# Sparse attention and gated feed-forward: block sums of the values on TensorE in column groups, a reordered start, other slots, stores on another queue

## Chip, cores, metric

One core of a Trainium2 chip runs the whole program. The metric is the device time of a run in microseconds (us); less is better. A ratio is the mean time of one kernel's fast runs over that of the kernel before in the same rounds on the same chip, so it is not quite the ratio of the medians that are quoted beside it.

In the profiles PE stands for TensorE's matmuls, PEld for its weight loads, DVE for VectorE, ACT for ScalarE, POOL for GpSimd, SP for SyncE; SPq and ACTq are instructions that start a DMA. L347 is a line of the kernel, x13 a number of instructions, and [2.30 <-DVE vx L427] says that the engine stood idle for 2.30 us and what ended it. The granted clock is the share of full TensorE speed that the chip allowed. PSUM is the memory that matmuls write to. A column group is the set of 32 of its 128 partitions that a small matmul writes to.

## The reference, cut to what matters

```python
batch, n_heads, seq, head_dim = (4, 8, 768, 64)
block, window = (32, 16)
k_sum = k.reshape(B, H, nb, block, D).max(axis=3)
v_sum = v.reshape(B, H, nb, block, D).mean(axis=3)        # block means: 24 per head
# scores: 15 neighbours on each side, and 24 block keys; one softmax over both
v_all = np.concatenate([v, v_sum], axis=2)
x = softmax(scores) @ v_all                               # -> 3072 tokens x 512
gate = 1.0 / (1.0 + np.exp(-(x @ w_gate)))
out = (gate * (x @ w_val)) @ w_out                        # d_ff = 1536
```

## The kernel before

Four batches go through one pipeline. While TensorE runs the feed-forward of batch b (24 units of 8 matmuls, then 12 output units of 6), the attention of batch b + 1 is put between its units: a text such as `6 Z0` means "after unit 6, do step Z of head pair 0". Each engine has one list of instructions, in the order of the program, so an instruction that waits can hold back those behind it on its engine (in the prediction's lines one wait stops all matmuls for 4.94 us). The step letters that matter here: T transposes keys and queries, K takes the key maxima (and spreads the keys), Z/S scores, A values, H halo copies, B spreads the block sums, D transposes by DMA.

```python
def sums(self, p, fill=0):          # batch 0: block sums on TensorE, all in column group 96:128
    vsp = self.vsp = ps([128, 512], FP32, "vsp")
    self.warm(vsp[:, 256:384], fill)            # fillers
    for t in range(NQ + 1):
        u = 2 * NQ * p + t
        nc.tensor.matmul(out=vsp[96:128, 0:128]..., lhsT=zband[0:64, 30 - 2 * t:62 - 2 * t],
                         rhs=self.vx[0:64, u:u + NQ + 1:NQ, 0:64], start=(t == 0), stop=(t == NQ))

def L(self, g, h=None, queue=None):  # batches 1 to 3: load the same values again, in fp32
    st = self.vm[g] = big()[0:4 * NS]
    (queue or nc.sync).dma_start(out=st, in_=v[self.b, 4 * g:4 * g + 4].rearrange(...))

def G(self, g, h):                   # ... reduce them on VectorE, put the result back by a small DMA
    nc.vector.tensor_reduce(out=self.mb[:, 32 * h:32 * h + 32], in_=self.vm[g]..., axis=AX.X, op=ALU.add)
    if h == 1:
        nc.sync.dma_start(out=self.heads(4 * g, 4 * g + 4, 0, 1, self.vx[96:120, ...]), in_=self.mb)

def m1(self, f, hf, c0=0, c1=NP):    # one feed-forward unit
    ...                              # 4 matmuls into gp, 4 into vp; four PSUM tiles: two units
    nc.scalar.activation(out=gate, in_=gp, func=ACT.Tanh, scale=0.5)
    nc.vector.scalar_tensor_tensor(out=self.hT[hf][:, f, :], in0=gate, scalar=1.0, in1=vp, ...)
...
NEXT = """
    3 T0   4 T1   5 Z0   6 T2   7 Z1   8 T3   9 G0a   10 Z2 G0b   11 G1a   12 Z3 G1b   13 H0 H1
    15 B0   16 B1   18 A0 A1   19 A2 A3 X0   20 X1   21 X2   22 X3"""
LATER = """
    0 G0a   1 G0b   2 K0   3 G1a   4 K1   5 G1b   6 Z0   8 K2 H0   10 Z1 H1   12 K3 B0   14 Z2 B1
    18 Z3   24 A0 A1   25 Y0   26 Y1   27 A2 A3   28 Y2   29 Y3"""
```

The start (batch 0 before its first complete feed-forward units) stands in an order of its own, with filler matmuls on a constant tile wherever TensorE would wait.

The softmax here doesn't subtract the row's maximum and nothing guards it: scores larger than these inputs give would overflow.

## Time and profile before

Median 261.63 us of three runs (259.44 to 261.75). The profiled span is 257.4 us. To compare kernels I cut the span at marks that can be read in the TensorE timeline: the end of the second complete feed-forward unit, and the first feed-forward matmul of the second half of batch 0 (45.32), of batch 1 (91.13), of batch 2 (151.66) and of batch 3 (206.60).

| stage, kernel before | us |
|---|---|
| start, to the end of two units | 26.21 |
| rest of batch 0's first half | 19.11 |
| batch 0, second half and output | 45.81 |
| batch 1 | 60.53 |
| batch 2 | 54.94 |
| batch 3 and end | 50.76 |

Batch 3 has no attention beside it: 46.9 us are matmuls without a wait, 3.9 us the last copy and store. Batches 1 and 2 carry some 3.6 us more matmuls, and no such end. The lines that carry the rest are in the prediction. The start, where fillers (L340) stand between the value steps (start, length, line, shapes):

```profile
15.21 0.90 PE L347 MATMUL vsp<-vx,zband 64*32 64x128 bf16 x13
16.04 0.38 PE L392 MATMUL av<-vs,P 24*64 24x64 bf16 x12
16.35 0.38 PE L377 MATMUL av<-vx,P 120*64 120x65 bf16 x12
16.66 0.62 PE L340 MATMUL last<-blank 128*128 128x128 bf16 x8
```

The fillers do nothing for the result. They take the place of idle time, and the granted clock is 1.00 through the start from its first record, at 3.94 us (before that 36 fillers come about 100 ns apart, later ones 57).

### The profile page before, as it was taken

The numbers are of one execution on the slowest core, as the hardware profiler recorded it, in microseconds if no ns is written. First come the engines' busy times: TensorE is split into PE (matmuls) and PEld (weight loads), VectorE is DVE, ScalarE is ACT, GpSimd is POOL, SyncE is SP. The second block draws the span as 40 slices with busy tenths as digits, with TensorE's granted clock in tenths as the row PEclk, the third lists the DMA queues.
The fourth block names the chain that finished last, engine by engine and source line by source line (L and its number), as shares of the span: only waits on it lengthen the run. The fifth ranks groups of instructions, "written<-read, shape, count | busy, mean of one in ns | idle before, by whom it ended". The sixth has DMA issues, their size and how long they took to land.

```text
span 257.4 us, 5546 instructions
## 1 busy us (share of the span) xinstructions
PE 239.9 (93%) x2290; PEld 137.8 (54%) x2290; DVE 149.8 (58%) x281; ACT 110.1 (43%) x193; POOL 65.4 (25%) x83
## 2 busy tenths in 40 slices
PE   8999999999996983998999999799999999999994
PEld 7687555566533541555555455455554456655441
DVE  7734857378997407999854219999654024444000
ACT  6833696488610450354541133455512233333111
POOL 8966434133899350262000000000000000000000
PEclk9999999999997997799999999999999999999999
DMA  7999999999999997999994963220006410000132
GB/s 186 147 158 196 203 204 222 221 167 126 125 125 160 166 228 169 161 177 162 133 87 80 173 173 105 35 63 3 1 3 175 122 72 0 3 0 0 43 122 82
DMA packets 87409, 30.74 MB, mean 119 GB/s; under 512 B 74520, under 2 KB 83736, under 8 KB 86808
## 3 DMA queue, kind: packets, MB, share of 16 engines
q0 software_dynamic: 62848, 15.37, 85.0%
q1 hardware_dynamic: 24536, 15.02, 27.5%
q8 instruction: 18, 0.29, 0.5%
q14 instruction: 7, 0.06, 0.1%
HBM read 33.08 MB, written 6.29 MB: 153 GB/s over the span
## 4 chain that ended last, share of the span: by engine, by line
PE 65%; DVE 14%; DMA 9%; issue 5%; ACT 4%; POOL 1%; SPq 1%; DVEq 0%; ACTq 0%; POOLq 0%
PE gp L498 18%; PE m L515 18%; PE vp L498 18%; DVE mb L417 4%; DMA vm<-in_v_dram 4%; DVE hT L506 3%; DVE P L327 2%; DMA k<-in_k_dram 2%; DMA vx<-mb 2%; ACT P L326 2%; PE av L444 2%; PE sc L320 2%; PE tp L205 2%; PE vsp L347 1%; PE last L340 1%
## 5 line engine op out<-in xcount | busy, mean ns | idle before, releaser
L506 DVE SCALAR_TENSOR_TENSOR hT<-gate,vp 128x384 bf16<-128x384 f32 x96 | 51.7, 549 | 59.1 <-PE vp L498 54.1
L498 PE MATMUL vp<-xT,wv 128*128 128x384 bf16 x384 | 80.1, 331 | 4.9 <-DVE hT L506 4.9
L498 PE MATMUL gp<-xT,wg 128*128 128x384 bf16 x384 | 80.3, 330 | 3.7 <-DVE hT L506 3.4
L505 ACT ACTIVATE gate<-gp 128x384 f32<-128x384 f32 x96 | 47.2, 493 | 64.2 <-PE gp L498 36.6
L515 PE MATMUL m<-wo,hT 128*128 128x512 bf16 x288 | 65.6, 384 | 0.0
L498 PEld LDWEIGHTS <-wv 128*128 128x128 bf16 x384 | 38.0, 99 | 30.9 <-issue 7.0
L498 PEld LDWEIGHTS <-wg 128*128 128x128 bf16 x384 | 36.0, 98 | 30.2 <-issue 8.4
L515 PEld LDWEIGHTS <-hT 128*128 128x128 bf16 x288 | 27.8, 99 | 32.1 <-issue 1.1
L520 ACT ACTIVATE ot<-m 128x512 f32<-128x512 f32 x24 | 14.3, 597 | 54.4 <-PE m L515 54.4
L417 DVE TENSOR_REDUCE mb<-vm 96x32 bf16<-96x1024 f32 x12 | 22.7, 1888 | 5.2 <-DMA vm<-in_v_dram 5.2
L326 ACT ACTIVATE P<-sc 128x768 bf16<-128x768 f32 x28 | 21.4, 812 | 6.1 <-PE sc L320 6.1
L161 POOL DMA_DIRECT2D vx<-in_v_dram x18 | 18.3, 1033 | 7.4 <-DMA nat<-in_q_dram 3.1
L155 POOL DMA_DIRECT2D nat<-in_q_dram x16 | 13.7, 857 | 21.6 <-DMA nat<-in_q_dram 12.7
L252 DVE TENSOR_REDUCE kTx<-kTn 128x24 bf16<-128x768 bf16 x16 | 15.1, 944 | 3.6 <-ACT kTn L210 3.6
L327 DVE TENSOR_TENSOR P<-P,mask 128x768 bf16<-128x768 bf16 x28 | 14.7, 550 | 3.3 <-ACT P L326 2.8
L155 POOL DMA_DIRECT2D nat<-in_k_dram x16 | 13.6, 853 | 9.9 <-DVE hT L506 3.7
L453 DVE TENSOR_TENSOR xs<-av,rec 128x768 bf16<-128x768 f32 (+1 forms) x16 | 13.7, 857 | 0.5
L444 PE MATMUL av<-vx,P 120*64 120x65 bf16 x336 | 8.2, 203 | 3.7 <-DVE vx L427 2.3
L444 PEld LDWEIGHTS <-P 120*64 120x64 bf16 x336 | 6.8, 117 | 7.7 <-issue 5.1
L474 ACT COPY xT<-br 128x384 bf16<-128x384 bf16 (+1 forms) x12 | 6.8, 587 | 9.5 <-PE br L471 9.5
L367 DVE COPY vx<-vx 32x792 bf16<-32x792 bf16 (+1 forms) x14 | 9.8, 705 | 0.3
L340 PEld LDWEIGHTS <-blank 128*128 128x128 bf16 x110 | 7.8, 111 | 2.4 <-DVE blank L567 1.1
(78 smaller groups left out, 140.2 us busy)
## 6 DMA issues: line engine op xcount, KB each, us to landing
out_dram<-ot SPq DMA_DIRECT2D x24, 256.0 KB, 2.1
vm<-in_v_dram SPq DMA_DIRECT2D x4, 768.0 KB
vx<-in_v_dram POOLq DMA_DIRECT2D x14, 192.0 KB, 14.7
wo<-in_moe_w_out_dram POOLq DMA_DIRECT2D x3, 512.0 KB, 21.0
vm<-in_v_dram POOLq DMA_DIRECT2D x2, 768.0 KB, 20.0
nat<-in_k_dram POOLq DMA_DIRECT2D x16, 96.0 KB, 10.8
nat<-in_q_dram POOLq DMA_DIRECT2D x16, 96.0 KB, 11.3
nat<-in_q_dram POOLq DMA_DIRECT2D x3, 384.0 KB, 14.0
```

What stands on the lines that cost most here:

```text
L155: nc.gpsimd.dma_start(out=nat[:, h // 2, :, 64 * (h % 2):64 * (h % 2) + 64], in_=tap[b, h].rearrange("(c p) d -> p c d", p=128))
L161: nc.gpsimd.dma_start(out=vx_t[b % 2][r0:r1, u0:u1, 0:64], in_=rows_of(v[b, 0, 0:1], (QT * u0 - 16 + r0) * D, [[D, r1 - r0], [QT * D, u1 - ...
L252: nc.vector.tensor_reduce(out=self.kTx[p][:, t, W:KX], in_=self.kTn[p][:, 16:16 + S].rearrange("p (n w) -> p n w", w=32), axis=AX.X, op=AL ...
L326: nc.scalar.activation(out=Ph, in_=sc[:, :, 0:6 * QT], func=ACT.Exp, scale=SCALE)
L327: nc.vector.tensor_tensor(out=Ph, in0=Ph, in1=mask[:, None, 6 * hf:6 * hf + 6, :].rearrange("p i t w -> p i (t w)") .to_broadcast([128, 2, ...
L417: nc.vector.tensor_reduce(out=self.mb[:, 32 * h:32 * h + 32], in_=self.vm[g].rearrange("p (w d) -> p d w", w=32)[:, 32 * h:32 * h + 32], a ...
L444: nc.tensor.matmul(out=av[r:r + 64, t // 6, (t % 6) // 2, i, 0:65], lhsT=P[0:KX, i, t, :], rhs=vx[0:KX, NQ * (2 * p + i) + t, 0:65], start ...
L498: nc.tensor.matmul(out=o, lhsT=wb[:, c, 128 * f:128 * (f + 1)], rhs=self.xT[:, c, HALF * hf:HALF * (hf + 1)], start=(c == 0), stop=(c == N ...
L505: nc.scalar.activation(out=gate, in_=gp, func=ACT.Tanh, scale=0.5)
L506: nc.vector.scalar_tensor_tensor(out=self.hT[hf][:, f, :], in0=gate, scalar=1.0, in1=vp, op0=ALU.add, op1=ALU.mult)
L515: nc.tensor.matmul(out=self.m3, lhsT=self.hT[hf][:, f, 128 * tt:128 * (tt + 1)], rhs=wo_bf[:, f], start=(f == 0), stop=(f == NF - 1))
L520: nc.scalar.mul(out=ot, in_=self.m3, mul=0.5)
```

## The change

The intent: no second, fp32 load of the values and no reduction on VectorE; all block sums as small matmuls in several column groups of TensorE at once; the value work of the first half batch between later scores in place of fillers; stores issued by ScalarE, so that SyncE's queue holds only transposes; the last tile in two halves. The diff, cut to its core (declarations and the order of some loads left out):

```diff
-        def L(self, g, h=None, queue=None): ...        # fp32 load
-        def G(self, g, h): ...                         # reduction, small DMA
+        def R(self, p, h=None):
+            vsp = ps([128, 512], FP32, "vsp")
+            for t in range(NQ + 1):
+                for p in range(NP):
+                    u = 2 * NQ * p + t
+                    nc.tensor.matmul(
+                        out=vsp[32 * p:32 * p + 32, 0:128].rearrange("p (h d) -> p h d", h=2),
+                        lhsT=zband[0:64, 30 - 2 * t:62 - 2 * t],
+                        rhs=self.vx[0:64, u:u + NQ + 1:NQ, 0:64],
+                        start=(t == 0), stop=(t == NQ), skip_group_check=True)
+            for p in range(NP):
+                nc.scalar.copy(out=vs[96:120, 2 * p:2 * p + 2], in_=vsp[32 * p:32 * p + 24, 0:128]...)
         def K(self, p, h=None):
             self.peaks(p)
+        def F(self, p, h=None):
             self.spread_keys(p, 0, NQ)
# S without its mask; M and N are the masks alone
-                nc.sync.dma_start(out=out[r:r + 128, :], in_=ot)
+                nc.scalar.dma_start(out=out[r:r + 128, :], in_=ot)
+        def last(self, part): ...     # last tile: 2 x (12 matmuls of 256 columns), each half copied
+                                      # half by ScalarE, half by VectorE, stored by SyncE
# start: values of heads 0,1 loaded before the last queries and keys; sums, near, far, transposes
# put between the scores of pairs 2 and 3; 48 of 110 fillers gone; pieces of units 0 and 1 instead
 LATER:
-        0 G0a   1 G0b   2 K0   3 G1a   4 K1   5 G1b   6 Z0   8 K2 H0   10 Z1 H1   12 K3 B0   14 Z2 B1
-        18 Z3   24 A0 A1   25 Y0   26 Y1   27 A2 A3   28 Y2   29 Y3
+        2 K0   3 F0   4 K1 Z0   5 F1   6 N0 Z1   7 K2   8 F2   9 N1 Z2   10 K3   11 F3   12 N2 Z3   13 H0
+        14 N3 R   16 H1   18 B0   20 B1   24 A0 A1   25 Y0   26 Y1 A2 A3   27 Y2   28 Y3
# the slots of batch 0 (REST, NEXT) changed likewise; batch 0's own sums: 64 columns, two groups
```

More of the change, by code (lines that the diff above doesn't have):

```diff
@@ L149, in load_nat @@
     def load_nat(b, h0, h1):
-        if h0 == 0:
+        if b > 2:
+            att[b].nat = att[b - 1].nat
+        elif h0 == 0:
             att[b].nat = [small().rearrange("p (a c d) -> p a c d", a=NP, c=6) for _ in range(2)]
@@ L233, in T @@
             self.natural(self.qT[p], at[:, 1])
-            self.K(p)
         def T1(self, p):
@@ L326, in S, with M @@
             nc.scalar.activation(out=Ph, in_=sc[:, :, 0:6 * QT], func=ACT.Exp, scale=SCALE)
+        def M(self, p, hf):
+            Ph = self.P[p][:, :, 6 * hf:6 * hf + 6, :].rearrange("p i t w -> p i (t w)")
             nc.vector.tensor_tensor(
@@ L335, in Z, with N, sums @@
             self.S(p, 1)
+        def N(self, p, h=None):
+            self.M(p, 0)
+            self.M(p, 1)
         def warm(self, out, n):
             for _ in range(n):
-                nc.tensor.matmul(out=out, lhsT=blank, rhs=blank, start=True, stop=True)
-        def sums(self, p, fill=0):
-            vsp = self.vsp = ps([128, 512], FP32, "vsp")
+                nc.tensor.matmul(out=out, lhsT=blank, rhs=blank[:, 0:out.shape[-1]], start=True, stop=True)
+        def sums(self, p, fill=0, vsp=None):
+            vsp = self.vsp = ps([128, 512], FP32, "vsp") if vsp is None else vsp
@@ L344, in sums @@
             self.warm(vsp[:, 256:384], fill)
             for t in range(NQ + 1):
-                u = 2 * NQ * p + t
-                nc.tensor.matmul(
-                    out=vsp[96:128, 0:128].rearrange("p (h d) -> p h d", h=2),
-                    lhsT=zband[0:64, 30 - 2 * t:62 - 2 * t],
-                    rhs=self.vx[0:64, u:u + NQ + 1:NQ, 0:64],
-                    start=(t == 0), stop=(t == NQ))
-        def means(self, p):
-            copy("act", vs[96:120, 2 * p:2 * p + 2], self.vsp[96:120, 0:128].rearrange("p (h d) -> p h d", h=2))
+                for i in range(2):
+                    nc.tensor.matmul(
+                        out=vsp[64 + 32 * i:96 + 32 * i, 0:64],
+                        lhsT=zband[0:64, 30 - 2 * t:62 - 2 * t],
+                        rhs=self.vx[0:64, NQ * (2 * p + i) + t, 0:64],
+                        start=(t == 0), stop=(t == NQ), skip_group_check=True)
@@ new lines, in means @@
+        def means(self, p):
+            for i in range(2):
+                nc.scalar.copy(out=vs[96:120, 2 * p + i], in_=self.vsp[64 + 32 * i:88 + 32 * i, 0:64])
+        def R(self, p, h=None):
[3 more added lines that the diff above has]
+                    u = 2 * NQ * p + t
+                    nc.tensor.matmul(
+                        out=vsp[32 * p:32 * p + 32, 0:128].rearrange("p (h d) -> p h d", h=2),
+                        lhsT=zband[0:64, 30 - 2 * t:62 - 2 * t],
+                        rhs=self.vx[0:64, u:u + NQ + 1:NQ, 0:64],
+                        start=(t == 0), stop=(t == NQ), skip_group_check=True)
+            for p in range(NP):
+                nc.scalar.copy(out=vs[96:120, 2 * p:2 * p + 2],
+                               in_=vsp[32 * p:32 * p + 24, 0:128].rearrange("p (h d) -> p h d", h=2))
@@ L369, in halo, with near @@
                 in_=self.heads(h0, h1, t0, t1, self.vx[0:32, 1:NU + 1]))
-        def near(self, p):
-            at = self.av[p] = ps([128, 512], FP32, "av")
+        def near(self, p, fill=0, at=None):
+            at = self.av[p] = ps([128, 512], FP32, "av") if at is None else at
+            self.warm(at[:, 396:512], fill)
             av = at[:, 0:396].rearrange("p (a i d) -> p a i d", a=3, i=2)
@@ L404, in far @@
             self.xs[p] = xs
-        def L(self, g, h=None, queue=None):
-            st = self.vm[g] = big()[0:4 * NS]
-            (queue or nc.sync).dma_start(
-                out=st,
-                in_=v[self.b, 4 * g:4 * g + 4].rearrange("h (n w) d -> n h (w d)", w=32))
-        def G(self, g, h):
-            if h == 0:
-                self.mb = vm_pool.tile([4 * NS, 64], BF16, name="mb", tag="mb")
-            with nc.allow_low_precision("sums kept in bf16 like the values"):
-                nc.vector.tensor_reduce(
-                    out=self.mb[:, 32 * h:32 * h + 32],
-                    in_=self.vm[g].rearrange("p (w d) -> p d w", w=32)[:, 32 * h:32 * h + 32],
-                    axis=AX.X, op=ALU.add)
-            if h == 1:
-                nc.sync.dma_start(
-                    out=self.heads(4 * g, 4 * g + 4, 0, 1, self.vx[96:120, 0:NU, 0:64])[:, :, 0], in_=self.mb)
         def B(self, g, h=None):
             nc.vector.tensor_copy(
-                out=self.heads(4 * g, 4 * g + 4, 1, NQ, self.vx[96:120, 0:NU]),
-                in_=self.heads(4 * g, 4 * g + 4, 0, 1, self.vx[96:120, 0:NU]).to_broadcast([NS, 4, NQ - 1, 66]))
+                out=self.heads(4 * g, 4 * g + 4, 0, NQ, self.vx[96:120, 0:NU, 0:64]),
+                in_=vs[96:120, 4 * g:4 * g + 4, None].to_broadcast([NS, 4, NQ, 64]))
         def H(self, g, h=None):
@@ L464, in Y, with X @@
                 in_=self.xs[p].rearrange("p c i d -> p (c i d)"))
-        def X(self, p, h=None):
+        def X(self, p, h=None, br=None):
             n = S if h is None else HALF
             o = 0 if h is None else HALF * h
-            br = ps([128, S], BF16, "br")
+            br = ps([128, S], BF16, "br") if br is None else br
             for qt in range(n // 128):
@@ L509, in m1, with last @@
             del self.open[f, hf]
+        def last(self, part):
+            r = self.b * S + S - 128
+            if part == 0:
+                self.m3 = [ps([128, 256], FP32, "m3") for _ in range(2)]
+                self.ot = ot_pool.tile([128, d_model], FP32, name="ot", tag="ot")
+            m3, ot = self.m3[part], self.ot
+            for f in range(NF):
+                nc.tensor.matmul(
+                    out=m3, lhsT=self.hT[1][:, f, 256:384], rhs=wo_bf[:, f, 256 * part:256 * part + 256],
+                    start=(f == 0), stop=(f == NF - 1))
+            c = 256 * part
+            nc.scalar.mul(out=ot[:, c:c + 128], in_=m3[:, 0:128], mul=0.5)
+            nc.vector.tensor_scalar_mul(out=ot[:, c + 128:c + 256], in0=m3[:, 128:256], scalar1=0.5)
+            nc.sync.dma_start(out=out[r:r + 128, c:c + 256], in_=ot[:, c:c + 256])
         def m2(self, hf, tt, part):
+            if (self.b, hf, tt) == (B - 1, 1, 2):
+                return self.last(part)
             if part == 0:
@@ L564 @@
     load_rows(k, 0, 4, 2, 0, S, k0[2])
+    load_v(0, 1, 25)
+    load_v(0, 0, 1, 16, 64)
     load_rows(q, 0, 4, 4, 0, HALF, q0[:, 0, 4:8])
     load_rows(k, 0, 6, 2, 0, S, k0[3])
+    load_v(0, 25, 49)
+    load_v(0, 49, 73)
+    load_v(0, 73, 97)
     nc.vector.memset(blank, 1.0)
@@ L570 @@
     nc.vector.memset(mask[W:128], 1.0)
-    load_v(0, 1, 25)
-    load_v(0, 0, 1, 16, 64)
-    load_v(0, 25, 49)
-    load_v(0, 49, 73)
-    load_v(0, 73, 97)
-    load_gates(0, 1)
-    load_gates(1, 1)
+    load_gates(0, 2)
+    load_gates(2, 2)
     load_rows(q, 0, 0, H, HALF, HALF, a0.q2)
-    load_gates(2, 2)
     load_gates(4, 2)
@@ L589 @@
         load_rows(q, 1, h, 4, 0, S, q1[:, h:h + 4])
-    load_wo(0, 4)
-    for g in range(2):
-        a1.L(g, queue=nc.gpsimd)
-    load_wo(4, 4)
-    load_wo(8, 4)
     nc.scalar.memzero(a0.heads(0, H, 0, 6, vx_t[0][96:128, 0:NU, 0:64]))
@@ L616 @@
     a0.S1(0, 0)
-    a0.fill = a0.sc[:, 1, 384:512]
     a0.T1(1)
@@ L622 @@
     a0.S1(0, 2)
-    a0.S1(1, 0, 4)
+    a0.S1(1, 0, 6)
     a0.S1(1, 1)
-    a0.T2(2, "act")
-    a0.T1(3)
     a0.S1(1, 2)
-    a0.S1(2, 0, 4)
-    a0.S1(2, 1)
-    a0.T2(3, "act")
-    a0.S1(2, 2)
-    a0.S1(3, 0, 4)
-    a0.S1(3, 1)
     a0.halo(0, 2, 0, 6)
@@ L636 @@
     a0.means(0)
-    a0.S1(3, 2)
-    idle = psum2.tile([128, 2, 512], FP32, name="last", tag="at")
-    a0.fill = idle[:, 0, 0:128]
     a0.near(0)
-    wait(6)
+    a0.T2(2, "act")
+    a0.S1(2, 0)
+    a0.far(0)
+    a0.S1(2, 1)
+    a0.T1(3)
+    a0.S1(2, 2)
     a0.halo(2, 4, 0, 6)
@@ L644 @@
     a0.means(1)
-    a0.far(0)
+    a0.T2(3, "act")
+    a0.X(0, 0)
+    a0.S1(3, 0)
     a0.near(1)
-    wait(8)
-    a0.X(0, 0)
     a0.far(1)
+    a0.S1(3, 1)
     a0.halo(4, 6, 0, 6)
@@ L652 @@
     a0.means(2)
-    wait(8)
+    a0.S1(3, 2)
     a0.near(2)
@@ L656 @@
     a0.far(2)
+    f0.m1(0, 0, 0, 1)
     a0.halo(6, 8, 0, 6)
-    a0.sums(3)
+    rest = psum2.tile([128, 2, 512], FP32, name="rest", tag="at")
+    a0.sums(3, 0, rest[:, 0])
     a0.means(3)
-    wait(6)
-    a0.near(3)
-    a0.X(2, 0)
+    f0.m1(0, 0, 1, 2)
+    a0.near(3, 0, rest[:, 1])
+    brs = psum2.tile([128, 2, 1024], BF16, name="brs", tag="at")
+    a0.X(2, 0, brs[:, 0])
     a0.far(3)
-    f0.m1(0, 0, 0, 1)
-    wait(6)
-    f0.m1(0, 0, 1, 2)
-    wait(6)
-    a0.X(3, 0)
+    f0.m1(1, 0, 0, 1)
+    f0.m1(1, 0, 1, 2)
     f0.m1(0, 0, 2, 3)
-    wait(8)
+    f0.m1(1, 0, 2, 3)
+    a0.X(3, 0, brs[:, 1])
+    a0.warm(rest[:, 0, 384:512], 6)
     a0.E(0)
@@ L673 @@
     f0.m1(0, 0, 3, 4)
+    f0.m1(1, 0, 3, 4)
     clear_ones(1)
     load_values(1)
-    def loads(b):
-        if b < B:
-            load_nat(b, 0, H)
-            load_values(b)
+    load_wo(0, 6)
+    load_wo(6, 6)
     REST = """
-        0 E1 I0   1 E2 Q0 I1   2 E3 Q1 Q2 I2   3 S0b Q3 I3   4 S1b U0   5 S2b U1   6 U2 S3b   7 U3 A0b
-        8 A1b   9 A2b A3b X0b   10 X1b X2b X3b"""
+        0 E1 I0   1 E2 I1 Q0 Q1   2 E3 I2 Q2 S0b   3 Q3 S1b M0b I3   4 S2b U0 M1b   5 S3b U1 M2b U2   6 M3b U3
+        7 A0b A1b   8 A2b A3b X0b X1b   9 X2b X3b"""
     NEXT = """
-        3 T0   4 T1   5 Z0   6 T2   7 Z1   8 T3   9 G0a   10 Z2 G0b   11 G1a   12 Z3 G1b   13 H0 H1
-        15 B0   16 B1   18 A0 A1   19 A2 A3 X0   20 X1   21 X2   22 X3"""
+        0 T0   1 K0   2 T1 F0   3 K1   4 T2 F1   5 K2   6 T3 F2   7 K3 Z0   8 F3 R   9 N0 Z1   10 H0   11 N1 Z2
+        12 H1   13 N2 Z3   14 B0   15 N3 B1   17 A0 A1   18 A2 A3   19 X0   20 X1   21 X2   22 X3"""
     LATER = """
-        0 G0a   1 G0b   2 K0   3 G1a   4 K1   5 G1b   6 Z0   8 K2 H0   10 Z1 H1   12 K3 B0   14 Z2 B1
-        18 Z3   24 A0 A1   25 Y0   26 Y1   27 A2 A3   28 Y2   29 Y3"""
+        2 K0   3 F0   4 K1 Z0   5 F1   6 N0 Z1   7 K2   8 F2   9 N1 Z2   10 K3   11 F3   12 N2 Z3   13 H0   14 N3 R
+        16 H1   18 B0   20 B1   24 A0 A1   25 Y0   26 Y1 A2 A3   27 Y2   28 Y3"""
     def add(at, text, a):
@@ L694, in add @@
             at.setdefault(i, []).extend(us)
-    run(f0.units1(0, 1), slots(REST, a0))
-    loads(2)
+    run(f0.units1(0, 2), slots(REST, a0))
+    load_nat(2, 0, H)
+    load_values(2)
     at = slots(NEXT, a1)
-    add(at, "13 D0   15 D1   17 L0 L1   20 D2   22 D3", att[2])
+    add(at, "17 D0   18 D1   20 D2   22 D3", att[2])
     run(f0.units1(1) + f0.units2(), at)
@@ L706 @@
         if b + 2 < B:
-            at[1].append(lambda: loads(b + 2))
-            add(at, "22 L0 L1   32 D0 D1", att[b + 2])
-        if b == 2:
-            add(at, "4 D2   6 D3", att[3])
+            at[0] = [lambda: load_nat(3, 0, H), lambda: load_values(3)]
+            add(at, "31 D0 D1   33 D2 D3", att[3])
         run(ffn.units1(0) + ffn.units1(1) + ffn.units2(), at)
```

## The prediction

> **What bounds the kernel now.** I read the page's busy shares and forty slices first, then the TensorE timeline, then the chain of waits, then VectorE and the DMA issues inside the stretches where TensorE's own row has holes.
>
> ```profile
> PE 239.9 (93%) x2290; PEld 137.8 (54%) x2290; DVE 149.8 (58%) x281; ACT 110.1 (43%) x193; POOL 65.4 (25%) x83
> PE   8999999999996983998999999799999999999994
> PEclk9999999999997997799999999999999999999999
> ```
>
> TensorE is the engine that sets the end, but its 93% hides two things: the span contains slices in which it is idle (12, 15) and slices in which the granted clock falls to 0.7 (12, 15, 16). The dense work is easy to price. In the timeline a block of four feed-forward matmuls follows the next by 0.65 us, and the last 72 output matmuls take 15.55 us in the chain, 0.216 us each. So 192 blocks are 124.8 us, 288 output matmuls 62.2 us, together 187.0 us of the 257.4 us span. The other 70 us are the start, the attention work and waits. To find the waits I list the TensorE timeline where the next start is later than the work before it explains:
>
> ```profile
> 76.37 0.25 PE L444 MATMUL av<-vx,P 120*64 120x65 bf16 x2
> 78.91 1.42 PE L444 MATMUL av<-vx,P 120*64 120x65 bf16 x46 [2.30 <-DVE vx L427]
> 80.26 2.53 PE L515 MATMUL m<-wo,hT 128*128 128x512 bf16 x6
> 82.97 0.57 PE L444 MATMUL av<-vx,P 120*64 120x65 bf16 x24 [0.18 <-DVE xs L453]
> 84.10 0.57 PE L444 MATMUL av<-vx,P 120*64 120x65 bf16 x24 [0.56 <-DVE xs L453]
> ...
> 95.03 0.81 PE L498 MATMUL gp<-xT,wg 128*128 128x384 bf16 x4
> 100.79 1.44 PE L498 MATMUL vp<-xT,wv 128*128 128x384 bf16 x4 [4.94 <-DVE hT L506]
> 102.02 1.48 PE L498 MATMUL gp<-xT,wg 128*128 128x384 bf16 x4
> ```
>
> First hole: from 76.37 to 84.60 stand 96 value matmuls (48 take 0.88 us later in the chain, so 1.76) and six output matmuls (1.30). That is 3.1 us of work in 8.2: 5.2 lost. Second: from 95.68 to 106.75 stand 20 feed-forward matmuls, 3.25 us of work in 11.1: 7.8 lost. Blocks take 1.28 us there, twice 0.65: the clock had fallen. Who caused them is told by the chain of waits (start, length, what):
>
> ```profile
> 73.31 1.84 DVE mb L417
> 75.17 5.13 DMA vx<-mb
> 80.33 1.33 DVE vx L427
> ...
> 85.13 1.25 SPq L222
> 87.05 11.34 DMA vm<-in_v_dram
> 98.59 1.60 issue
> ```
>
> Both lead to the fp32 block sums: VectorE reduces (L417), the result goes through a small DMA of 5.1 us, VectorE spreads it; and the next fp32 load is issued late on SyncE's queue, behind transposes and stores, and takes 11.3 us. VectorE, in order, stands before its reduction and so cannot free the PSUM tiles of the feed-forward.
>
> The third loss is many small waits in the feed-forward of batches 1 and 2. Windows (busy and count of PE, PEld, DVE, ACT, POOL, then clock, DMA, GB/s) show VectorE full:
>
> ```profile
> 155.00:160.00 5.00, 4.79 (x29) 2.64 (x28) 5.00 (x8) 1.96 (x4) 0.00 (x0) 1.00 0.14 50
> 160.00:165.00 5.00, 4.06 (x45) 2.37 (x45) 5.00 (x8) 2.39 (x4) 0.00 (x0) 1.00 0.50 84
> ```
>
> From 151.66 to 189.08 there are 48 blocks (31.2 us) and four score groups (0.46 each): 33.0 of 37.4 us, 4.4 lost. In batch 1, from 106.75 to 128.94, 28 blocks and four score groups are 20.0 of 22.2: 2.2 lost.
>
> **What the Trainium skill says.** "TensorE: Matmul & The Clock Gate", Part 1, states that an idle window of about 3.4 us puts the array back to half clock. This trace agrees: after the 5 us hole the blocks take 1.28 instead of 0.65 us, in a stretch of granted clock 0.50. The same page, Part 3, states that small matmuls in different column groups run concurrently. The trace supports it indirectly: value matmuls, which alternate between two column groups, come at 0.88/48 = 18 ns with 65 columns, while the sums, all in one group with 128 columns, take 0.83/13 = 64 ns. "VectorE: DVE Perf Modes", the perf-mode tier table, gives reductions no fast mode; here one of 96x1024 costs 1.89 us. "DMA: Bandwidth & Descriptors", "Issuing engines are not separate DMA queues", says stores moved to another queue still share the same 16 engines; so I price that move by SyncE's queueing alone, not as bandwidth.
>
> **The change, part by part.**
>
> *Removed.* Twelve reductions, 22.7 us of VectorE; six fp32 loads of 768 KB; six small DMAs; 48 of 110 filler matmuls. Two of the loads stand in GpSimd's load stream: they land at 50.8 and 54.5 us, after the load that landed at 46.3, so everything behind them moves up by 8.2 us. The next values landed at 60.7 to 65.7 and now go ahead of the output weights too: about 44 to 49 us. They are wanted at feed-forward slot 8 of that stage, near 58 us, so they are there.
>
> *Added.* Three times 52 sum matmuls in four column groups. At the measured floor of 18 ns they cost 1.0 us, allowing for mode changes 1.2 us; if they ran one after the other at 64 ns, 3.3 us. ScalarE gets four copies of about 0.26 us each time, and 22 store issues. The spreading copy now writes 3072 elements for 2904, from a tile in place of a landed DMA: about 1 us as now.
>
> *The start.* I walk the TensorE order with the durations of the trace. First scores are unchanged to about 9.7 us. The values of heads 0 and 1 move ahead of two loads and should land near 9.3 instead of 12.0; the second values stay near 13.9, as everything before them in the stream has the same bytes. So the first value work slips in near 10 to 11 us, the second starts at 14.0, the third near 16.5. The first gate weights still land near 19.9 (two loads of two tiles in place of four of one, the same bytes), a wait of some 1.5 us at the first feed-forward piece; then sums, values and transposes to about 24.6 us for two complete units. Before, the second unit ended at 26.21. Gain 1.6. The rest of batch 0's first half has the same work with one unit less behind; with masks kept apart from scores I give it 0.6 more.
>
> *Batch 0, second half, 45.3 to 91.1 now.* The 5.2 us fall away; 1.2 come in for the sums, and I leave 0.8 for value groups that wait on the two PSUM tiles they share. Gain 3.2.
>
> *Batch 1, 91.1 to 151.7 now.* The work is 31.2 + 1.84 + 1.76 + 15.55 = 50.4 us in 60.5. New: 50.4 + 1.2 sums + 1.0 left over = 52.6. Gain 7.9. VectorE can keep up: slots 2 to 16 hold 15 products (0.54), four key maxima (0.94) and spreads (0.67), eight masks (0.5) and two halos (1.1), 20.7 us against some 23 of TensorE.
>
> *Batch 2.* 54.9 now, 50.4 + 1.2 + 0.9 = 52.5. Gain 2.4.
>
> *Batch 3.* No attention; unchanged but for its end. The final ScalarE copy of 0.60 us falls to about 0.3 (half on VectorE), the store is half as big. Gain 0.5.
>
> Sum: 1.6 + 0.6 + 3.2 + 7.9 + 2.4 + 0.5 = 16.2 us, which leaves a span near 241.2 and, taken from the median of 261.63, a time of 245.4 us.
>
> **Rivals.** *Sums serialise on TensorE.* For it: 156 more matmuls on the bounding engine, each with its weight load. Against: the 18 ns of two-group value matmuls. It would take back 3 x 2.1 = 6 us: about 251.5. *A new wait on VectorE.* Without the reductions it still does a product, a maximum and a spread per unit, 1.3 to 1.5 us in some slots against 1.3; four PSUM tiles cover only two units. For: the small waits in batch 1. Against: the sum over the slots. It would leave 2 us in each of two batches: about 249. *Loads bound the first 35 us.* Gates for units 9 to 11 land near 34.6 whatever the order; if the start got much faster than I think, they would stop it, so the start can gain at most some 4 us. *Stores on ScalarE hold its copies up.* An issue took SyncE 0.33 to 0.57 us; during output matmuls ScalarE has 0.6 of work per 2.6 us, and some transposes' copies of 0.8. Worth 1 us at most. *The holes are replaced by a DMA wait elsewhere*, such as transposed keys of the next batch: they are issued later than now (slot 17 for 13), but their loads should land near 67 us for 76. Would cost 2 to 5 us.
>
> **Range and chances.** The two large holes, 13 us, have one cause each, and the change takes both away; that carries the sign. What is soft is the start (0 to 4 us), the sums (0 to 6 us against me) and small waits (2 us either way). I predict 245.5 us, 8 in 10 between 241 and 251.5. Faster by over 2% means under 256.4: 0.95; within 2%: 0.04; slower: 0.01.
>
> **What will show it.** In the changed profile the granted clock stays at 1.00 after 25 us and no hole of TensorE exceeds 2 us; the lines of L417 and the fp32 loads of values are gone; the 52 sums of one batch stand in about 1.2 us (3 us would be the first rival); two complete feed-forward units stand at about 24.6 us; batches 1 and 2 take some 52.5 us each; VectorE falls to about 128 us busy. It is wrong if TensorE waits for VectorE's products for more than 3 us in a batch, if a new DMA wait of over 3 us appears, or if the start is not shorter.

## The result, and the profile after

The changed kernel takes 248.86 us (median of four, 248.18 to 249.33) for 260.86; the ratio is 0.9543, 95% interval 0.9484 to 0.9601. That lies inside the predicted range and 3.4 us above the predicted 245.5. Span: 247.5 us for 257.4; the predicted span was 241.2.

The busy shares, and the slices of TensorE and its granted clock, of the changed kernel:

```profile
PE 237.2 (96%) x2462; PEld 138.2 (56%) x2462; DVE 130.1 (53%) x271; ACT 113.6 (46%) x210; POOL 62.0 (25%) x78
...
PE   7889999799999999999999999999999999999993
...
PEclk9995799999999999999999999999999999999998
```

The holes of slices 12 and 15 (counted from 0) are gone, and so are their low clocks. But a low clock stands in slices 3 and 4 now, where the kernel before had none. TensorE's timeline at the place of the old first hole:

```profile
78.97 0.95 PE L452 MATMUL av<-vx,P 120*64 120x65 bf16 x48
79.86 1.47 PE L541 MATMUL m<-wo,hT 128*128 128x512 bf16 x6
81.26 0.57 PE L452 MATMUL av<-vx,P 120*64 120x65 bf16 x24
82.01 0.57 PE L452 MATMUL av<-vx,P 120*64 120x65 bf16 x24 [0.18 <-DVE xs L461]
```

The 96 value matmuls and six output matmuls take 3.6 us from 78.97, where they took 8.2. The block sums of a whole batch are one line:

```profile
64.66 0.92 PE L373 MATMUL vsp<-vx,zband 64*32 64x128 bf16 x52
```

The next matmuls start at 65.51, so they cost 0.85 us. The windows of the start (busy time and count of PE, PEld, DVE, ACT, POOL; granted clock; DMA; GB/s) show the loss:

```profile
15.00:20.00 5.00, 4.70 (x123) 3.40 (x115) 1.94 (x5) 3.06 (x9) 2.44 (x4) 0.75 1.81 177
20.00:25.00 5.00, 5.00 (x65) 2.77 (x62) 2.09 (x7) 1.02 (x4) 2.32 (x4) 0.50 1.51 197
25.00:30.00 5.00, 4.91 (x28) 2.88 (x26) 1.66 (x6) 1.84 (x4) 2.22 (x3) 0.72 1.33 201
```

TensorE is "busy" for all of 20 to 25 us, at half clock. Read alone, that busy share looks perfect; only the clock column tells that each matmul takes longer. In the kernel before, the same three windows have a clock of 1.00.

Stage by stage, with the predicted change of each:

| stage | before | changed | predicted change | measured change |
|---|---|---|---|---|
| start, to the end of two units | 26.21 | 28.29 | -1.6 | +2.1 |
| rest of the first half | 19.11 | 19.89 | -0.6 | +0.8 |
| batch 0, second half | 45.81 | 42.16 | -3.2 | -3.65 |
| batch 1 | 60.53 | 53.28 | -7.9 | -7.25 |
| batch 2 | 54.94 | 52.73 | -2.4 | -2.2 |
| batch 3 and end | 50.76 | 51.17 | -0.5 | +0.4 |
| sum | 257.36 | 247.52 | -16.2 | -9.8 |

So the middle came as predicted, within 0.7 us in each stage. The start, the rest of the first half and the end had the wrong sign. The 0.4 us of the end are no more than that stage, with the same code, differs between profiles (next section).

### The profile page after: what moved, and what is told of

Same layout as the page of the kernel before. It is cut to its first block, busy times and chain, and to the rows that moved or that the text cites. A ratio compares the mean times of both kernels' runs of the same rounds, so it can differ in the third digit from the quotient of the medians.

```text
span 247.5 us, 5885 instructions
## 1 busy us (share of the span) xinstructions
PE 237.2 (96%) x2462; PEld 138.2 (56%) x2462; DVE 130.1 (53%) x271; ACT 113.6 (46%) x210; POOL 62.0 (25%) x78
## 3 DMA queue, kind: packets, MB, share of 16 engines
q1 hardware_dynamic: 20288, 5.77, 13.7%
## 4 chain that ended last, share of the span: by engine, by line
PE 78%; DVE 7%; issue 5%; ACT 4%; DMA 3%; POOL 2%; DVEq 0%; POOLq 0%
PE m L541 24%; PE gp L506 21%; PE vp L506 20%; DMA vx<-in_v_dram 3%; DVE hT L514 3%; PE sc L323 3%; PE av L452 2%; ACT gate L513 2%; PE tp L207 2%; DVE xs L461 1%; ACT P L329 1%; DVE kTx L260 1%; PE br L479 1%; PE m L527 1%; PE vsp L373 1%
## 5 line engine op out<-in xcount | busy, mean ns | idle before, releaser
L514 DVE SCALAR_TENSOR_TENSOR hT<-gate,vp 128x384 bf16<-128x384 f32 x96 | 53.0, 553 | 80.2 <-ACT gate L513 51.2
L541 PE MATMUL m<-wo,hT 128*128 128x512 bf16 x276 | 62.1, 379 | 0.0
L541 PEld LDWEIGHTS <-hT 128*128 128x128 bf16 x276 | 26.1, 98 | 29.8
L546 ACT ACTIVATE ot<-m 128x512 f32<-128x512 f32 x23 | 13.7, 597 | 49.4 <-PE m L541 43.4
L163 POOL DMA_DIRECT2D vx<-in_v_dram x18 | 17.4, 986 | 4.5 <-DMA wg<-in_moe_w_gate_dram 2.7
L157 POOL DMA_DIRECT2D nat<-in_k_dram x16 | 13.7, 859 | 14.0 <-DMA vx<-in_v_dram 7.8
L157 POOL DMA_DIRECT2D nat<-in_q_dram x16 | 14.6, 910 | 10.2 <-DMA vx<-in_v_dram 6.3
L461 DVE TENSOR_TENSOR xs<-av,rec 128x768 bf16<-128x768 f32 (+1 forms) x16 | 13.7, 858 | 0.6
L323 PEld LDWEIGHTS <-kTx 64*128 64x128 bf16 x336 | 6.3, 95 | 6.4 <-DVE kTx L260 3.4
L393 DVE COPY vx<-vx 32x792 bf16<-32x792 bf16 (+1 forms) x14 | 9.0, 645 | 1.1 <-DMA vx<-in_v_dram 0.8
L323 PE MATMUL sc<-qT,kTx 64*128 64x64 bf16 x336 | 8.6, 191 | 0.9 <-DVE kTx L260 0.3
L452 PE MATMUL av<-vx,P 120*64 120x65 bf16 x336 | 7.2, 196 | 1.8 <-DVE xs L461 1.8
```

The lines of the kernel that those rows point to most:

```text
L157: nc.gpsimd.dma_start(out=nat[:, h // 2, :, 64 * (h % 2):64 * (h % 2) + 64], in_=tap[b, h].rearrange("(c p) d -> p c d", p=128))
L163: nc.gpsimd.dma_start(out=vx_t[b % 2][r0:r1, u0:u1, 0:64], in_=rows_of(v[b, 0, 0:1], (QT * u0 - 16 + r0) * D, [[D, r1 - r0], [QT * D, u1 - ...
L323: nc.tensor.matmul(out=sc[:, i, QT * t6:QT * (t6 + 1)], lhsT=kTx[64 * i:64 * i + 64, t, :], rhs=qT[64 * i:64 * i + 64, QT * t:QT * (t + 1) ...
L452: nc.tensor.matmul(out=av[r:r + 64, t // 6, (t % 6) // 2, i, 0:65], lhsT=P[0:KX, i, t, :], rhs=vx[0:KX, NQ * (2 * p + i) + t, 0:65], start ...
L461: nc.vector.tensor_tensor(out=xs[:, 0:3 * G].rearrange("p (g a) i d -> p g (a i) d", g=G), in0=avf[:, :, :, 0:64], in1=rec[:, 0:G].to_broa ...
L541: nc.tensor.matmul(out=self.m3, lhsT=self.hT[hf][:, f, 128 * tt:128 * (tt + 1)], rhs=wo_bf[:, f], start=(f == 0), stop=(f == NF - 1))
```

## The experiments

Twelve runs were made, in three groups of four, each group on a chip of its own with its own runs of the kernel before; two of the twelve repeat e2 and e9, one the changed kernel. The stages of all of them, from their profiles:

| kernel | time us | ratio | start | rest | b0, 2nd | b1 | b2 | b3, end |
|---|---|---|---|---|---|---|---|---|
| c1_again (changed) | 249.24 | 0.953 | 29.72 | 19.64 | 42.16 | 53.23 | 52.73 | 51.15 |
| e1_fill | 250.11 | 0.9566 | 28.47 | 19.90 | 42.14 | 53.24 | 52.71 | 51.16 |
| e2_sums_only | 244.45 | 0.934 | 26.61 | 19.11 | 42.06 | 51.80 | 51.81 | 51.21 |
| e3_one_group | 252.92 | 0.9665 | 27.54 | 19.89 | 43.69 | 54.79 | 54.26 | 51.15 |
| e8_new_slots | 247.41 | 0.9492 | 27.08 | 19.10 | 41.99 | 53.55 | 52.72 | 51.20 |
| e9_new_start | 245.26 | 0.9416 | 25.93 | 19.92 | 42.22 | 51.81 | 51.81 | 50.91 |
| e10_stores_last | 244.26 | 0.9373 | 28.00 | 19.10 | 42.07 | 51.80 | 51.81 | 51.12 |
| e5_load_first | 261.92 | 1.0044 | 26.64 | 19.10 | 47.40 | 60.43 | 54.94 | 50.75 |
| e12_scores_later | 244.96 | 0.9402 | 26.74 | 19.10 | 41.99 | 51.91 | 51.92 | 51.19 |
| e6_no_load | 253.22 | 0.9712 | 27.46 | 19.10 | 44.69 | 54.96 | 54.93 | 50.52 |
| e2_again | 244.63 | 0.9377 | 26.64 | 19.10 | 42.07 | 51.81 | 51.81 | 51.19 |
| e9_again | 245.22 | 0.9426 | 26.94 | 19.92 | 42.22 | 51.81 | 51.81 | 50.92 |

The time is the median of the fast runs, the stages are those of the one profiled run. The middle stages repeat within 0.3 us when their code is the same. The last stage has the same code in the kernel before, e5, e6 and e2, and reads 50.52 to 51.21 us there. The start of the old order ranges from 26.2 to 28.0 us by itself, so its time must not be read from a single profile.

**c1_again: the changed kernel once more.** No edit.

> The changed kernel unaltered, as a control on the same chip: 248 to 250 us, ratio to the kernel before 0.95 to 0.96. If the half-clock stretch in its start (17.5 to 27.8 us in the first trace) is a property of the kernel and not of that one run, it is there again, 7 to 10 us long.

The half clock is there again, for 13.65 us, longer than the 7 to 10 expected, and two units end at 29.72. It belongs to the kernel, but its length changes.

**e1_fill: fillers back in the start of the changed kernel.**

```diff
-    a0.sums(1)
+    a0.sums(1, 10)
-    a0.near(1)
+    a0.near(1, 5)
# the tile rest is taken earlier for this
+    a0.warm(rest[:, 0, 384:512], 6)     # before near(2)
+    a0.warm(rest[:, 0, 384:512], 20)    # after far(2)
```

> The changed kernel with 41 filler matmuls (56 ns each at full clock, 2.3 us if none lay in a wait) put back where TensorE waits in the start. Theory A (the clock falls to half at 17.5 us because the start has holes and only narrow matmuls without the fillers): the granted clock stays 1.00 through the start, the first two feed-forward units end near 25 us in place of 28.5, the span falls by some 3 us, time near 246. Theory B (the start is long because of late loads, the clock only makes the waits look busy): units end at 28 to 29 us all the same, the time is 249 to 251.

Neither theory came out whole. The half clock shrank to one stretch of 3.41 us, so the fillers do act on the clock. Yet two units end at 28.47 and the time is 250.11. The profile says why: the clock fell just ahead of the twenty fillers, which then ran at half clock.

```profile
20.65 2.31 PE L350 MATMUL rest<-blank 128*128 128x128 bf16 x20
```

As a repair this is a failure; as a test of the clock it is only half a test.

**e2_sums_only: the kernel before with the TensorE sums of batches 1 to 3, nothing else of the change.**

```diff
-        def L(...), def G(...)
+        def R(...)                       # as in the change
-    NEXT:  9 G0a   10 Z2 G0b   11 G1a   12 Z3 G1b
+    NEXT:  10 Z2   11 R   12 Z3
-    LATER: 0 G0a   1 G0b   2 K0   3 G1a   4 K1   5 G1b   6 Z0   8 K2 H0   10 Z1 H1   12 K3 B0
+    LATER: 2 K0   4 K1   6 Z0   8 K2 H0   10 Z1 H1 R   12 K3 B0
```

> The kernel before with one part of the change alone: block sums of batches 1 to 3 on TensorE in four column groups, no fp32 value loads; start, store queue, masks and last tile as before. Theory A (the two holes and the small waits come from the fp32 sums and their loads; the new start is no gain): both holes gone, first two units at 26.2 us as before, time 245 to 248, so at least as fast as the changed kernel. Theory B (the moved start, masks and stores carry a good part): time 252 or more.

Theory A, and more than it asked: 244.45 us, 4.8 us faster than the changed kernel beside it. Two lines of its page:

```profile
span 242.6 us, 5823 instructions
...
PE   8999999899999999999999999999999999999992
```

Batches 1 and 2 are at 51.8 us. This is also the version that beats both kernels. So the other parts of the change together cost time, and the next runs put them back one at a time.

**e3_one_group: the same sums, one column group after the other.**

```diff
-            for t in range(NQ + 1):
-                for p in range(NP):
+            for p in range(NP):
+                for t in range(NQ + 1):
```

> The changed kernel with the 52 sums of a batch ordered one column group after the other instead of in turn; same instructions. If column groups run side by side, each batch's sums go from 0.85 us (first trace) to about 3.3 us (64 ns each as in the kernel before), the time rises by 3 x 2.4 = 7 us to about 256. If the 0.85 us comes from something else (128-column sums that are just cheap behind other work), the time stays within 1 us of the changed kernel.

```profile
114.29 2.46 PE L373 MATMUL vsp<-vx,zband 64*32 64x128 bf16 x52
```

The same 52 instructions take 2.46 us in place of 0.92; each of the three stages grows by 1.5 us, and the time by 3.7 (less than three times 1.5: these runs had a little more clock, 0.980 to 0.986 for 0.969 to 0.982 in c1_again). That column groups run side by side is shown. The size that I gave was too large: I took 64 ns a matmul from the start of the kernel before, here they come at 2.46/52 = 47 ns. The edit also makes neighbours add into the same rows of PSUM. That is no rival: feed-forward matmuls do the same at 0.65/4 us for 384 columns, 0.42 ns a column, and these take no longer, 0.37.

**e8_new_slots: e2 plus the new slots of batches 1 to 3** (masks and spreads as units, later transposes, the shared buffer).

```diff
-    LATER: 2 K0   4 K1   6 Z0   8 K2 H0   10 Z1 H1 R   ...
+    LATER: 2 K0   3 F0   4 K1 Z0   5 F1   6 N0 Z1   7 K2   8 F2   9 N1 Z2   10 K3   11 F3   12 N2 Z3   ...
```

> The kernel with TensorE sums alone (244.45 us), plus the change's new slots for batches 1 to 3: masks and key spreads as units of their own, later transposes, the shared buffer of the last batch. Theory A (the new slots put a score group one unit after the key spread that it needs, so TensorE waits on VectorE): batches 1 and 2 take 53.3 and 52.7 us as in the changed kernel instead of 51.8 each, time 246 to 247.5. Theory B (the new slots help and the changed kernel's longer batches come from its stores on ScalarE or its ending): batches stay at 51.8 or less, time 243 to 244.5.

Theory A: batches 1 and 2 grow by 1.75 and 0.91 us, the time by 3.0. TensorE at the third group of scores of batch 1, and, in the second fence, VectorE (DVE) before it:

```profile
103.15 0.20 PE L323 MATMUL sc<-qT,kTx 64*128 64x64 bf16 x2 [0.16 <-DVE kTx L260]
103.78 0.49 PE L323 MATMUL sc<-qT,kTx 64*128 64x64 bf16 x22 [0.43 <-DVE hT L512]
```

```profile
102.17 0.55 DVE L512 SCALAR_TENSOR_TENSOR hT<-gate,vp 128x384 bf16<-128x384 f32 x1
102.64 0.45 DVE L260 COPY kTx<-kTn 128x1152 bf16<-128x1152 bf16 x1
103.01 0.72 DVE L261 COPY kTx<-kTx 128x264 bf16<-128x264 bf16 x1
```

The spread of the keys (L260, L261) stands on VectorE behind the product of the unit before it; the scores that read it stand one unit later on TensorE. The spread ends after TensorE has got there. (The profile names L512 for the second wait; it ends at 103.72, the spread L261, which the scores read, at 103.73.) No engine is full: this is a distance that is too short.

**e12_scores_later: e8 with every score group two units after its spread.**

```diff
-        2 K0   3 F0   4 K1 Z0   5 F1   6 N0 Z1   7 K2   8 F2   9 N1 Z2   10 K3   11 F3   12 N2 Z3   13 H0   14 N3 R
+        2 K0   3 F0   4 K1   5 F1 Z0   6 N0   7 K2 Z1   8 F2   9 N1   10 K3 Z2   11 F3   12 N2   13 H0 Z3   14 R   15 N3
```

> The kernel with TensorE sums and the new slots (247.41 us; batches 1 and 2 at 53.55 and 52.72 us), with each score group moved to two units after the key spread that it reads instead of one. If the new slots lose because the scores wait for that spread, batches 1 and 2 fall to 52 us or less and the time to 244 to 245.5. If the loss comes from the masks or spreads being units of their own, or from the transposes, the batches stay above 52.5 us and the time at 247.

Batches 1 and 2 fall to 51.91 and 51.92 us, the time to 244.96. So the slots lost by that distance (R and N3 changed places too); 0.1 us is left. Masks and spreads of their own neither help nor harm.

**e9_new_start and e9_again: e2 plus the new start**, with everything after the first half batch as in e2.

> The kernel with TensorE sums alone (244.45 us), plus the change's new start: the order of the first loads, value work between scores, fewer fillers, the slots of the first half batch. Theory A (the start loses by itself: half clock and a late end): first two units end at 27.5 to 29.7 us instead of 26.6, the rest of the first half takes 19.6 to 19.9 instead of 19.1, later batches stay at 51.8, time 246 to 248.5. Theory B (the start is late in the changed kernel only through something later in the load stream or the stores): it ends at or before 26.6 and the time is 244.5 or less.

> The kernel with TensorE sums alone, again, as the base for the next run on the same chip: 244 to 245 us, ratio 0.933 to 0.940, no half clock in the start.

> The same with the change's new start, again, with more rounds, to settle what the start is worth. Theory A (the start loses by itself, by 1 to 3 us, through half clock of a length that changes from run to run): ratio to the kernel before higher than that of the run beside it by 0.004 to 0.012, half clock for 3 to 14 us before 30 us. Theory B (no difference): the two ratios within 0.003 of each other.

The first run left it open (four times from 244.36 to 246.81). With more rounds beside e2 on the same chip the ratio is 0.9426 for 0.9377, a difference of 0.0049 or 1.3 us, though the two intervals overlap and the medians are only 0.6 us apart. What settles the mechanism is the granted clock of the single runs. With the old start (e2_again) all five lie at 0.997 to 1.000 and 243.86 to 244.85 us. With the new start the six runs are:

```
time us        244.44  244.74  245.02  245.41  246.81  247.93
granted clock   0.993   0.992   0.986   0.986   0.979   0.969
```

The time follows the clock: 3.5 us for 0.024. Carried on to 1.000 it would be some 243.4 us, an estimate from these six, so the new order as such would gain about 1 us and loses it and more through the clock. The window of the profiled run:

```profile
20.00:25.00 5.00, 5.00 (x57) 2.70 (x52) 1.44 (x6) 0.88 (x3) 2.45 (x4) 0.50 1.49 197
```

Six profiles were taken with the new start, and all have a half-clock stretch between 15 and 30 us, 3.4 to 13.7 us long. Eight were taken with the old start, and none has one there. (One of the six is e1_fill, with its fillers.)

The kept traces say more. Every half-clock stretch inside them is 1, 2, 3 or 4 times 3.41 us, so I looked at the 3.41 us just before each fall:

| profile | TensorE busy in the 3.41 us before, us | longest wait in it | half clock, us | two units end |
|---|---|---|---|---|
| e9_new_start | 2.50 | 0.75 | 3.41 | 25.93 |
| e1_fill (own fillers) | 2.46 | 0.77 | 3.41 | 28.47 |
| e9_again | 2.45 | 0.93 | 6.83 | 26.94 |
| e3_one_group | 2.40 | 0.98 | 6.83 | 27.54 |
| changed | 2.66 | 0.30 | 10.24 | 28.29 |
| c1_again | 1.88 | 1.53 | 13.65 | 29.72 |

So TensorE was busy for 55 to 78% of it; between 11 and 28 us the eight profiles of the old start have no such window with less than 3.2 us busy. Several waits, none over 1.53 us, make up the rest; in four of the six the longest is for a load (values or gate weights). Busy time is not the whole rule: three windows of 69 to 76% between 3.9 and 10.1 us (changed, e6, e10) were not followed by a fall. Which part of the new start makes the waits (fewer fillers, narrower sums, later loads) was not taken apart and stays open. Without e1_fill, the last column is fitted by a line that meets zero half clock at 24.7 us: an estimate from five profiles, in which a longer wait for loads may move both columns.

The rest of the first half is 19.92 us with the new start, and 19.10 in e8, which has the masks apart but the old slots. So the 0.8 us belong to the new slots of that half (or to what they inherit from the new start), not to the masks. In the changed kernel it is two waits of the last value groups, which share two PSUM tiles:

```profile
45.10 0.38 PE L452 MATMUL av<-vx,P 120*64 120x65 bf16 x12 [1.19 <-DVE xs L461]
45.89 0.38 PE L452 MATMUL av<-vx,P 120*64 120x65 bf16 x12 [0.40 <-DVE xs L461]
```

**e10_stores_last: e2 plus stores on ScalarE's queue and the last tile in halves.**

```diff
-                nc.sync.dma_start(out=out[r:r + 128, :], in_=ot)
+                nc.scalar.dma_start(out=out[r:r + 128, :], in_=ot)
+        def last(self, part): ...        # as in the change
```

> The kernel with TensorE sums alone (244.45 us), plus stores on ScalarE's queue and the last tile in halves. What I predicted before: 0.5 us faster (243.9). Theory from the trace of the changed kernel (VectorE's half of each last copy waits for ScalarE's half, 0.28 + 0.29 us one after the other, and SyncE's queue holds nobody up once the fp32 loads are gone): no gain, 244 to 245 us, and from the end of TensorE to the end of the span 4.2 to 4.3 us as without.

No gain: 244.26 for 244.45 and 244.63. From the end of TensorE to the end of the span it is 4.18 us here, 4.30 in e2 and 3.86 in the kernel before; what made e2's end longer than that is not known. The end of the changed kernel shows the term that I got wrong:

```profile
242.64 1.66 SPq L533 DMA_DIRECT2D out_dram<-ot  x2
243.32 0.28 ACT L531 ACTIVATE ot<-m 128x128 f32<-128x128 f32 x1 [1.03 <-PE m L527]
243.63 0.29 DVE L532 TENSOR_SCALAR ot<-m 128x128 f32<-128x128 f32 x1 [1.02 <-ACT ot L531]
```

VectorE's half waits for ScalarE's half: 0.28 + 0.29 us one after the other, against one copy of 0.60 before. Both read one PSUM tile and write one output tile; which of the two makes the wait no run tells.

**e5_load_first: the kernel before, the two fp32 loads of batch 2 issued ahead of the transposes.**

```diff
-    add(at, "13 D0   15 D1   17 L0 L1   20 D2   22 D3", att[2])
+    add(at, "12 L0 L1   13 D0   15 D1   20 D2   22 D3", att[2])
```

> The kernel before with one edit: the two fp32 value loads of batch 2 are issued ahead of the key and query transposes on SyncE's queue (slot 12 for 17), nothing removed. Theory A (the second hole of 7.8 us is only a late issue): the wait of VectorE for that load (5.2 us) goes, the half-clock stretch at 99.5 us with it, time 254 to 256. Theory B (the loads as such crowd the DMA engines, whatever their order): the transposes or the values of the next batch come later, a hole opens elsewhere, time within 2 us of the kernel before.

Theory B. The time is 261.92 us, the hole of batch 1 is still there, with another name on it:

```profile
99.52 1.44 PE L498 MATMUL vp<-xT,wv 128*128 128x384 bf16 x4 [3.73 <-ACT ot L520]
```

```profile
81.84 6.98 SPq L222 DMA_TRANSPOSE qT<-nat  x1
88.91 0.53 SPq L522 DMA_DIRECT2D out_dram<-ot  x1
89.55 3.58 SPq L222 DMA_TRANSPOSE kTn<-nat  x1
93.31 2.58 SPq L222 DMA_TRANSPOSE qT<-nat  x1
95.98 1.01 SPq L522 DMA_DIRECT2D out_dram<-ot  x2
```

Now the transposes are late, the stores stand behind them on SyncE's queue, and ScalarE waits 4.8 us for an output tile to be stored before it can do the next gate. A late issue was one way in which these loads hurt, not the cause.

**e6_no_load: the kernel before, reductions kept, fp32 loads left out** (they read a tile that was cleared once; the result is wrong).

```diff
-            st = self.vm[g] = big()[0:4 * NS]
-            (queue or nc.sync).dma_start(out=st, in_=v[...])
+            if "st" not in keep:
+                keep["st"] = big()
+                nc.vector.memset(keep["st"], 0.0)
+            self.vm[g] = keep["st"][0:4 * NS]
```

> The kernel before with the reductions, the small DMA of their results and the spreading kept, but reducing from a tile that is cleared once: no fp32 value loads at all (the result is wrong on purpose). Theory A (the first hole is the small DMA and what follows it, the second the fp32 load, the small waits the time of VectorE): the second hole and its half clock go, the first shrinks by at most half, batch 2 stays near 54.9 us; time 250 to 254. Theory B (VectorE's 1.9 us reductions make the holes): both holes stay within 2 us of their size, time 258 or more. Theory C (the loads make all of it): time 246 or less, as with the sums on TensorE.

Theory A by its numbers: 253.22 us, batch 1 down to 54.96, batch 2 at 54.93 as before. It also divides the gain of e2. Against the kernel before, leaving out the loads alone takes 1.1, 5.6 and 0.0 us off the three stages: 6.7 us. Taking away the reductions and the small DMA as well (e2) takes off another 2.6, 3.2 and 3.1: 8.9 us, with 0.85 us of sums for each batch already paid. But one reading of mine falls. The first hole is still there, and the chain of waits behind it holds no DMA:

```profile
72.07 1.82 DVE mb L418
73.89 0.93 DVE P L328 x2
74.82 1.82 DVE mb L418
76.64 0.03 issue
76.67 2.17 DVE vx L368 x2
78.84 0.03 issue
78.87 1.11 DVE vx L428
```

The two reductions push the halo copies (L368) and the spread (L428) behind them on VectorE, and TensorE waits for the spread. In the kernel before, the small DMA ran beside the halo copies (2.35 us) and the first spread (1.31) for most of its 5.13 us; only the second spread waited for it, 1.46 us.

## Why the prediction was right, and where it was not

**The two holes and the small waits: right.** The step "Both lead to the fp32 block sums" holds: with those sums gone and nothing else changed (e2), the stages of batches 0 to 2 shrink by 3.75, 8.73 and 3.13 us. I had given 3.2, 7.9 and 2.4. The changed kernel itself reached 3.65, 7.25 and 2.2.

**Who made the holes: partly right.** For the first I named the small DMA of 5.1 us together with the reductions; e6 shows that VectorE's own queue is enough to make it. For the second I wrote that the load "is issued late on SyncE's queue"; e5 shows that issuing it early moves the wait to the stores, while e6 shows that leaving it out removes it. The sign did not depend on this, since the change took away all of it: that the two causes had not been told apart cost nothing here, which is luck.

**The sums: right in kind, over-sized.** Predicted 1.2 us per batch, measured 0.85. The rival "Sums serialise on TensorE" is answered by e3: side by side they take 0.92 us, in turn 2.46, so even the bad case would have cost 1.5 us per batch and not 2.1.

**The start: wrong sign.** The step that failed is "I walk the TensorE order with the durations of the trace": those durations are of full clock, and I let the fillers go as if they were only waits. I quoted the rule of the clock for the holes and did not ask it of the part of the kernel from which the change takes 48 fillers. The trace that I quoted held a warning: the clock fell at the first hole too, after a wait of only 2.30 us (TensorE was busy for 1.11 of the 3.41 us before), so a full idle window is not needed. Two units ended at 28.29 and 29.72 us for 24.6 predicted; 10.2 and 13.7 us of it ran at half clock. At full clock the walk itself may have been right: the line above points to 24.7 us. My range for the start (a gain of 0 to 4 us) did not hold a loss. The rival "Loads bound the first 35 us" was not tested, since the start did not get faster.

**Rest of the first half: wrong sign, small.** I gave 0.6 us to the masks; e8 and e9 show that the masks do nothing and that the new slots cost 0.8.

**Small waits of batches 1 and 2: mis-sized.** "VectorE can keep up: slots 2 to 16 hold" was a sum over slots, and by that sum it does. What it could not see is the distance: a spread on VectorE and the scores that read it one unit apart. That is 1.75 and 0.9 us (e8), and two units of distance give it back (e12). I had left 1.0 and 0.9 for all waits left over. It is the rival "A new wait on VectorE", which I had named with 2 us in each batch and thought unlikely because of that sum.

**Stores and end: the gain of 0.5 us did not come.** The two halves of the last copies run one after the other, and moving the stores is worth nothing measurable once the fp32 loads are gone (e10). The other 0.4 us are not theirs: e2 has them too, without this edit. The rival "Stores on ScalarE hold its copies up" cost nothing either: in e10 the issues stand on ScalarE and the stages are those of e2.

**No new DMA wait:** right. The transposed keys came in time, and the values of batch 1 landed between 45.15 and 51.08 us (predicted 44 to 49; their sums start at 64.66, not near 58).

**Its own signs of being wrong.** One of three came: the start is not shorter. The clock was to be at 1.00 after 25 us and was at half until 27.78. The others held: no later wait of TensorE over 1.19 us, VectorE at 130.1 us for 128.

**The total: in part luck.** The stages sum to 9.8 us for 16.2, and the span missed its 241.2 by 6.3 us, the time only by 3.4. The gains were read from the profile of a run of 259.25 us (span 257.4) and taken off the median of 261.63.

From e2 to the changed kernel the parts add up: 244.5, plus 3.0 for the slots, 1.3 for the start, 0 for stores and end, is 248.8; measured 248.86 and 249.24. That fit is closer than its terms: e8's profile has 0.5 us of its 3.0 in the start, whose code it did not change, and the start of the changed kernel had more half clock than e9's profiles.

## What to carry to other kernels

When a change bundles several ideas, price and test each alone: here one of them was worth more than the whole, and two of the others gave a quarter of it back. Before filler work on TensorE is removed, ask whether what takes its place keeps the granted clock up; read the clock beside the busy share, which says 100% at half speed. And a producer on one in-order engine must stand far enough ahead of its consumer on another: sums of busy time over a stretch do not show a distance that is one unit too short.

## What the Trainium skill lacked or had wrong

- "TensorE: Matmul & The Clock Gate", Part 1, ties the fall to half clock to an idle window of about 3.4 us; a later passage of the same part has a clock that goes back and forth because TensorE idles briefly between groups of matmuls, without an amount. Here the clock fell after stretches of 3.41 us with TensorE busy for 55 to 78% and no wait over 1.53 us (0.30 in the changed kernel), and in the kernel before after one with 1.11 us busy. How much work keeps the clock up neither passage says; these runs do not settle it, since three stretches of 69 to 76% passed without a fall.
- The same page, Part 3, gives speedups of column groups for matmuls of 512 columns; for 64 rows, 32 columns out and 128 columns in, accumulating, no page has a measured number. Here four groups in turn take 0.92 us for 52 and one after the other 2.46, a factor of 2.7.
- Part 1 says that the number of slow matmuls at the start of a kernel differs from run to run; no page has how much a later stretch can differ. Here one kernel ran at 0.969 to 0.993 mean granted clock over six runs, and 3.5 us went with it.
